# A transformer block with dilated local attention: softmax on tiles transposed by DMA, V scratch kept per block

## The chip, the cores and the metric

The kernel runs on one core of a Trainium2 chip. A core has TensorE (PE in the profile; its weight loads are listed apart as PEld), VectorE (DVE), ScalarE (ACT), GpSimd (POOL) and SyncE (SP), which issues most of the DMA transfers, and sixteen DMA engines that carry them out. The metric is the device time of one execution in microseconds, as the median of several runs.

## The reference

An adaptive layer norm block over x with 2048 positions and 512 channels, bf16: attention with 32 heads of 16 channels in which each position looks at eight earlier ones, two apart, and then a gated feed-forward of width 1792.

```python
mod = (_silu(c) @ w_mod).reshape(c.shape[0], 6, 1, -1)
sa, ca, ga, sb, cb, gb = (mod[:, i] for i in range(6))
h = _layernorm(x) * (1 + ca) + sa
x = x + ga * attention(h)          # below
h = _layernorm(x) * (1 + cb) + sb
x = x + gb * ((gelu(h @ w_gate) * (h @ w_up)) @ w_down)

# attention: W, dil = 8, 2
idx = pos[:, None] - (jnp.arange(W) * dil)[None, :]
kg, vg = k[:, :, idx], v[:, :, idx]              # idx < 0 masked
logits = jnp.einsum('bhsd,bhswd->bhsw', q, kg) * Dh ** (-0.5)
attn = _softmax(jnp.where(idx >= 0, logits, -1e9))
o = jnp.einsum('bhsw,bhswd->bhsd', attn, vg)     # then @ wo
```

## The kernel before, in words

The 2048 positions are worked in four blocks of 512 (sg = 0 to 3). For a block the steps are: layer norm (st, mv, rstd on POOL, xn; L404 to L419), a transposition of xn to channels on partitions (hT; in block 0 by TensorE, L432, in the others by a DMA transposition, L439), scale and shift by the modulation (L447), twelve qkv tiles of four matmuls each (L491) with copies by ScalarE to qT, kT and vT, the logits as products pq = qT * kT shifted by 2w on VectorE (L541) summed over channels by TensorE (LTp, L555), the softmax, the products pv of the probabilities with V on VectorE (L658) summed by TensorE (o_ps, L670), the output projection (x1, L690), the second layer norm and its transposition (h2, also L439), and the feed-forward: g and u (L718), gelu and a copy by ScalarE (L742, L749), their product hh on VectorE (L760), the down projection y (L731) and the store.

In the products pv the four window positions w4 of a group sit on four groups of 32 partitions, so V has to be there four times, each copy shifted by 2*w4 positions. That is done through DRAM: vT is stored to a scratch vscr (L518), and four loads of 32 partitions each read it back with the four shifts into the tile V4 (L527), one run of 520 positions for each of 16 rows of a partition. V4 has one buffer, so the loads of a block wait until the products pv of the block before are done. For block 0, which has nothing before its first position, POOL clears the edge (L240).

The softmax takes the logits LT, with window and head on partitions, transposes them with TensorE into PSUM (LNp, L587), takes the maximum (L598) and subtracts it (z, L607) on VectorE, takes exp on ScalarE (L614), then sum, reciprocal and product on VectorE (L621, L626, L631), transposes back with TensorE (PTp, L640) and copies to PT with ScalarE (L646).

The order of the instructions on every engine is fixed when the program is built. A planner steps through the threads of all blocks; each Op names its engine, a duration, the events it waits for, the buffers it takes and gives back, and the table PR gives each thread a priority. Among the steps that can begin at nearly the same time (within the slack of the engine), the one of lowest priority number goes first. All loads except three are issued by SP from one list (sp_q), mixed with the stores and the DMA transpositions; the first three, c and two parts of w_mod, go through ScalarE's queue. On each queue instructions run strictly in the planned order. PSUM's eight banks are split into four for matmul results (mm), two for attention (att) and two for transposes (tp).

Of the kernel before, what the change touches and what calls it, by code (L numbers as in the profile page):

```python
# [17 lines left out]
PR = {  # L18
    "ga": 28, "mb": 30.4, "gb": -2.8, "wds": 56.8, "wos": 73.9, "ln1": [33.1, 16.9, 32.7, 29.1], "t1": [-35.2,
    55, 3.9, 6.5], "h1": [4.7, 2.3, 4.2, 1], "qkv": [15, 5.4, 30.8, 36], "qev": [40, 53.9, 9, 22.7], "v":  # L20
    [14.4, 70, 13, 46.1], "pq": [7.4, 84.3, 109.8, 154.6], "lmm": [4.5, 21.5, -2.4, 5.1], "lev": [2.2, 19.8,
    38.5, 5.6], "smm": [4.6, 25, 3, -0.9], "soft": [23, 19.5, 1.7, 8.3], "e": [64, 19.2, 103, 16], "ptp": [8,
    7.1, -1.7, 4.8], "pt": [-10.8, 0.2, 10.5, 42.3], "pv": [2.4, 11.1, 71.1, 29.2], "pvmm": [35.5, 31.3, 3.8,
    4.1], "pvev": [-14.5, 64.7, 32.1, 40], "x1mm": [18.6, 1.6, -24.2, -9.1], "x1": [-12.8, 1.5, -0.7, -2],
    "ln2": [28.5, 36.7, 1.4, 68.5], "t2": [1.8, -14.8, 3.9, 0.1], "h2": [-1, 17.3, -2, 10.1], "ffn": [45.9,
    18, 20.7, 56.2], "act": [30.1, -13.5, -2.2, 57.1], "hh": [-5.2, -5.3, 0, 14.6], "st": [150.1, 14.3, 34.2,
    31.2],
# [14 lines left out]
class Op:  # L42


    def __init__(self, eng, w, fn, after=(), take=(), give=(), fire=None, lat=None, act=None, pr=None, dma=None,
                 quad=False):
# [3 lines left out]
        self.quad = quad  # L50


class Planner:
# [5 lines left out]
    def __init__(self):  # L59
        self.clock = {e: 0.0 for e in self.LAT}  # L60
        self.threads = []
        self.done = {}
        self.slack = {"PE": 0.51, "ACT": 0.68, "DVE": 0.14, "POOL": 0, "SP": 0}
        self.far = {"PE": 0, "ACT": 0.05, "DVE": 0.21, "POOL": 0, "SP": 0}
        self.table = None
        self.quad = False
        self.dma = 0.0
        self.log = []
# [4 lines left out]
    def _begin(self, th):  # L73
        op, last = th[2], th[3]
        t = max(self.clock[op.eng], th[4])
        if last is not None:
            t = max(t, last)
        for name in op.after:
# [9 lines left out]
    def run(self):  # L88
# [5 lines left out]
        while live:  # L94
# [27 lines left out]
            if op.dma:  # L122
                self.dma = max(self.dma, t) + (op.lat or 0.0)
                fin = max(end, self.dma) + self.LAT["SP"]
# [4 lines left out]
            if op.fire:  # L129
                self.done[op.fire] = fin  # L130
            self.log.append((t, end, eng, op.fire, th[0]))
# [8 lines left out]
def kernel(  # L140
# [24 lines left out]
    VR = S + VH  # L165

    def pool(name, bufs, **kw):
# [5 lines left out]
          "wm": 1, "hh": 16, "o": 2, "wA": 1, "mm": 4, "att": 2, "tp": 2}  # L173
    pools = {k: pool(k + "_p", NB[k]) for k in NB if k not in ("mm", "att", "tp", "wm")}
    for k in ("mm", "att", "tp"):
# [5 lines left out]
    vscr = dram.tile([P, 4, VR], BF16, name="vscr")  # L181
# [646 lines left out]
```

## Time and profile before

| quantity | value |
|---|---|
| median of 3 runs (lowest, highest) | 254.66 us (254.41, 255.35) |
| profiled execution: its own time | 255.11 us |
| profiled execution: span | 253.2 us |
| busy: PE, DVE, ACT, POOL | 240.3, 185.2, 144.6, 15.3 us |
| granted TensorE clock over the span | 0.987 |
| DMA: packets, volume | 37417, 29.41 MB |
| V loads: number and size, median us from issue to landing | 12 of 520 KB, 9.7 |
| first qkv matmul, first pv product | 13.27 us, 49.16 us |

The span is the profiled stretch of the core; the execution's own time is 1.9 us longer. A busy share is the share of the span in which the engine has an instruction under way; matmuls overlap, so a row's count times its mean duration exceeds its busy time. Where a row names "idle before", that is time in which the engine waited, and the name behind the arrow is what ended the wait. The chain is followed back from the last instruction, at each step to what released it. In the rows of SP's queue the duration is the time that the issuing instruction held the queue, not the transfer's.

### The profile page before, as it was taken

Reading aid. Unit: us, or ns where it says so; the run is one execution under the profiler, and the core shown is the slowest. Engines: PE = TensorE matmul, PEld = TensorE weight load, DVE = VectorE, ACT = ScalarE, POOL = GpSimd, SP = SyncE. Lnnn points to the kernel's source line nnn. Section 1 sums busy time; section 2 is a strip of 40 time slices with the busy share of each in tenths; the row PEclk is TensorE's granted clock in tenths of the full one; section 3 lists DMA queues with packets and bytes.
Section 4 is the critical chain, followed back from the end, with each engine's and each line's share of the span. In section 5 each row is a group of like instructions: output and inputs, shape, how many; then the busy total and the mean of one; then the engine's idle time right before and its main releaser. Section 6 shows DMA issues by size and latency. Waiting matters only on the chain.

```text
span 253.2 us, 3608 instructions
## 1 busy us (share of the span) xinstructions
PE 240.3 (95%) x1353; PEld 105.2 (42%) x1353; DVE 185.2 (73%) x295; ACT 144.6 (57%) x237; POOL 15.3 (6%) x37
## 2 busy tenths in 40 slices
PE   6789698899999999999999999999999999999994
PEld 2444334434443433444444334444344444444441
DVE  3499949999999999999999969688948422222221
ACT  2065459978569967430796763448654730766400
POOL 3410003000200000002000001000001000000000
PEclk9799979999999999999999999999999999999999
DMA  6999899999983500973300069510000401000011
GB/s 213 350 332 283 166 193 188 356 346 255 198 190 116 183 0 0 203 137 71 81 16 1 0 129 197 116 43 23 0 0 3 84 21 52 11 4 0 0 41 41
DMA packets 37417, 29.41 MB, mean 116 GB/s; under 512 B 15512, under 2 KB 36248, under 8 KB 37400
## 3 DMA queue, kind: packets, MB, share of 16 engines
q1 hardware_dynamic: 36336, 28.14, 47.2%
q10 hardware_dynamic: 1064, 1.05, 1.3%
q8 instruction: 10, 0.16, 0.3%
q14 instruction: 7, 0.06, 0.1%
HBM read 21.32 MB, written 4.19 MB: 101 GB/s over the span
## 4 chain that ended last, share of the span: by engine, by line
PE 71%; DMA 14%; DVE 7%; ACT 5%; SPq 1%; issue 1%; DVEq 0%; ACTq 0%
PE y_ps L731 19%; PE g_ps L718 19%; PE u_ps L718 19%; DMA wm<-in_w_mod_dram 5%; PE x_ps L690 5%; PE qkv_ps L491 4%; PE o_ps L670 3%; DMA x<-in_A_x_dram 3%; DMA hT<-xn 3%; DMA h<-xn 2%; DVE st L404 2%; DVE pq L541 2%; ACT hT L447 1%; PE LTp L555 1%; ACT h L447 1%; DVE xn L419 1%
## 5 line engine op out<-in xcount | busy, mean ns | idle before, releaser
L718 PE MATMUL g_ps<-h,Wg 128*128 128x512 bf16 x224 | 57.9, 379 | 0.6 <-ACT h L447 0.3
L718 PE MATMUL u_ps<-h,Wu 128*128 128x512 bf16 x224 | 57.6, 379 | 0.0
L491 PE MATMUL qkv_ps<-hT,wqkv 128*128 128x512 bf16 x192 | 47.3, 390 | 3.9 <-ACT hT L447 2.6
L731 PE MATMUL y_ps<-WdP,hht 128*128 128x512 bf16 x224 | 49.3, 379 | 0.0
L742 ACT ACTIVATE gl<-g_ps 128x512 bf16<-128x512 f32 x56 | 33.5, 599 | 26.7 <-PE g_ps L718 23.3
L749 ACT CAST ub<-u_ps 128x512 bf16<-128x512 f32 x56 | 33.0, 588 | 20.2 <-PE u_ps L718 20.2
L760 DVE TENSOR_TENSOR hht<-gl,ub 128x512 bf16<-128x512 bf16 x56 | 23.5, 420 | 28.1 <-ACT ub L749 27.5
L658 DVE TENSOR_TENSOR pv<-PT,V 128x2048 bf16<-128x2048 bf16 x32 | 37.8, 1219 | 1.0 <-ACT PT L646 1.0
L541 DVE TENSOR_TENSOR pq<-qT,kT 128x2048 bf16<-128x2048 bf16 x32 | 37.8, 1216 | 0.4 <-ACT kT L508 0.4
L718 PEld LDWEIGHTS <-Wg 128*128 128x128 bf16 x224 | 21.1, 98 | 28.5 <-issue 4.6
L731 PEld LDWEIGHTS <-hht 128*128 128x128 bf16 x224 | 21.8, 98 | 26.4 <-issue 0.4
L718 PEld LDWEIGHTS <-Wu 128*128 128x128 bf16 x224 | 21.1, 98 | 27.7 <-issue 4.0
L491 PEld LDWEIGHTS <-wqkv 128*128 128x128 bf16 x192 | 20.9, 115 | 26.5 <-issue 9.8
L404 DVE BATCH_NORM_STATS2 st<-x 128x6 f32<-128x512 bf16 x32 | 21.7, 680 | 6.4 <-DMA x<-in_A_x_dram 6.3
L767 DVE TENSOR_TENSOR ot<-y_ps,x 128x512 bf16<-128x512 f32 x16 | 11.0, 687 | 21.1 <-PE y_ps L731 21.1
L413 POOL TENSOR_TENSOR rstd<-rstd,neghalf 128x4 f32<-128x4 f32 x8 | 10.7, 1340 | 178.9 <-DVE rstd L409 178.9
L447 ACT ACTIVATE h<-h,modT,scl 128x512 bf16<-128x512 bf16 x16 | 11.7, 803 | 7.1 <-DMA h<-xn 7.0
L690 PE MATMUL x_ps<-woP,oT 128*128 128x512 bf16 x64 | 15.6, 379 | 0.0
L508 ACT CAST kT<-qkv_ps 128x512 bf16<-128x512 f32 x16 | 9.2, 586 | 5.8 <-PE qkv_ps L491 5.8
L419 DVE TENSOR_SCALAR xn<-x,mv,rstd 128x512 bf16<-128x512 bf16 x32 | 11.4, 408 | 1.6 <-POOL rstd L413 1.5
L512 ACT CAST vT<-qkv_ps 128x512 bf16<-128x512 f32 x16 | 9.4, 588 | 5.2 <-PE qkv_ps L491 5.1
L699 DVE TENSOR_TENSOR x<-x_ps,x 128x512 bf16<-128x512 f32 x16 | 10.8, 683 | 1.7 <-PE x_ps L690 1.5
(62 smaller groups left out, 157.7 us busy)
## 6 DMA issues: line engine op xcount, KB each, us to landing
V<-vscr SPq DMA_DIRECT2D x12, 520.0 KB, 9.7
wm<-in_w_mod_dram SPq DMA_DIRECT2D x4, 512.0 KB, 9.8
vscr<-vT SPq DMA_DIRECT2D x4, 512.0 KB, 7.1
out_dram<-ot SPq DMA_DIRECT2D x16, 128.0 KB, 1.7
Wg<-in_B_w_gate_dram SPq DMA_DIRECT2D x1, 1792.0 KB, 7.5
Wu<-in_B_w_up_dram SPq DMA_DIRECT2D x1, 1792.0 KB, 11.9
WdP<-in_B_w_down_dram SPq DMA_DIRECT2D x1, 1792.0 KB, 7.5
wqkv<-in_A_wqkv_dram SPq DMA_DIRECT2D x3, 512.0 KB, 7.4
```

The lines of the kernel that those rows point to most:

```text
L404: nc.vector.bn_stats(out=st_k["st"][:, c4, :], in_=src()[:, c4, :])
L419: nc.vector.tensor_scalar(out=B[key][:, c4, :], in0=src()[:, c4, :], scalar1=st_k["mv"][:, c4, 0:1], scalar2=st_k["rstd"][:, c4:c4 + 1], o ...
L447: nc.scalar.activation(out=h, in_=h, func=ACT.Identity, scale=sc(dt), bias=bi(dt))
L491: nc.tensor.matmul(ps[:].rearrange("p (c k) -> p c k", k=P), lhsT=wqkv[:, dt, blk * D + j:(blk + 1) * D:4], rhs=B["hT", sg][:, :, dt, :], ...
L541: nc.vector.tensor_tensor(out=pq[:], in0=_ap(B["qT", sg][:, j, :], [[0, 4], [1, SG]]), in1=_ap(kT[:, j, k0:k0 + SG], [[2, 4], [1, SG]]), o ...
L658: nc.vector.tensor_tensor(out=t[:], in0=_ap(B["PT", sg][:, wg, :], [[0, 4], [1, SG]]), in1=B["V4", sg][:, :, j, c0:c0 + SG], op=ALU.mult)
L690: nc.tensor.matmul(ps[:], lhsT=B["oT", sg][:, j, c4 * P:(c4 + 1) * P], rhs=woP[:, j, :], start=(j == 0), stop=(j == 3))
L718: nc.tensor.matmul(ps[:].rearrange("p (c k) -> p c k", k=P), lhsT=Wt[:, dt, ft * P:(ft + 1) * P], rhs=B["h2T", sg][:, :, dt, :], start=(dt ...
L731: nc.tensor.matmul(ps[:], lhsT=B["hh", sg, ft][:, c4 * P:(c4 + 1) * P], rhs=B["WdP"][:, ft, :], start=(ft == 0), stop=(ft == FT - 1))
L742: nc.scalar.activation(out=gl[:], in_=B["g", sg, ft][:], func=ACT.Gelu_apprx_tanh)
L749: nc.scalar.copy(out=ub[:], in_=B["u", sg, ft][:])
L760: nc.vector.tensor_tensor(out=hh[:], in0=B["gl", sg, ft][:], in1=B["ub", sg, ft][:], op=ALU.mult)
```

## The change

Five things are changed together.

1. **V scratch.** Every block has a scratch of its own, vscr[sg], with a halo of 16 positions in front (VL = 528 positions a row). POOL writes the halo into vT (zeros for block 0, the last 16 positions of the block before for the others; vhalo), the store writes the whole tile, and each of the four loads reads a partition's 16 rows as one contiguous stretch of 8448 - 2*w4 elements and writes it 2*w4 elements further on. The loads pass max_dma_last_dim=4 * VL.
2. **Softmax.** LT is transposed by a DMA transposition on SP (soft_in), not by TensorE, into a bf16 tile LN in SBUF; maximum and sum are trees of elementwise operations in three levels; subtraction, exp and the product with the reciprocal work in place; the result goes back by a second DMA transposition (soft_out).
3. **PSUM.** The pool tp is gone; mm has five banks and att three.
4. **Loads and weights.** wqkv lies in SBUF by its three parts; the loads are several threads with priorities of their own (q_head, q_wo, q_x, q_mb, q_gu, q_gb, q_d), all on SP except c.
5. **Head.** x of block 0 comes in two loads, its layer norm is finished in two halves, its transposes are ordered by halves (transp0), warm-up matmuls are moved and three are added. The planner has new priorities, slacks and durations; a step with hold keeps SP occupied until its transfer is over.

The diff, without the table of priorities and without edits that only carry names:

```diff
@@ Planner._begin
+        if op.dma:
+            t = max(t, self.lanes[0])
@@ Planner.run
-                fin = max(end, self.dma) + self.LAT["SP"]
+                if op.hold:
+                    end = self.clock[eng] = max(end, self.dma)
+                fin = max(end if not op.hold else 0.0, self.dma) + self.LAT["SP"]
+                self.lanes = self.lanes[1:] + [fin]
...
-    VR = S + VH
+    VL = SG + VH
-          "wm": 1, "hh": 16, "o": 2, "wA": 1, "mm": 4, "att": 2, "tp": 2}
+          "wm": 1, "hh": 16, "o": 2, "wA": 1, "mm": 5, "att": 3, "ln": 1, "PT": 1}
-    vscr = dram.tile([P, 4, VR], BF16, name="vscr")
+    vscr = [dram.tile([P, 4, VL], BF16, name=f"vscr{g}") for g in range(NSG)]
-    wqkv = pools["wA"].tile([P, DT, 3 * D], BF16, name="wqkv", tag="wA")
+    wqkv = pools["wA"].tile([P, 3, DT, D], BF16, name="wqkv", tag="wA")
...
+        def q_head():
+            yield Op("SP", 0.45, ldx(0, 0, 1), fire="x0.0", lat=mb(0.125))
+            yield Op("SP", 0.45, ldx(0, 1, 4), fire="x0.1", lat=mb(0.375))
+            yield Op("SP", 0.5, ldwm(1), take=[SL[WM[1]]], fire="wm1", lat=mb(0.5))
+            yield Op("SP", 0.5, ldwm(0), take=[SL[WM[0]]], fire="wm0", lat=mb(0.5))
+            yield Op("SP", 0.5, ldq(0), fire="wqkv0", lat=mb(0.5))
+            yield Op("SP", 0.5, ldq(1), fire="wqkv1", lat=mb(0.5))
+            yield Op("SP", 0.5, ldx(1), fire="x1", lat=mb(0.5))
+            yield Op("SP", 0.5, ldq(2), fire="wqkv2", lat=mb(0.5))
+            yield Op("SP", 0.5, ldx(ORDER[2]), fire=f"x{ORDER[2]}", lat=mb(0.5))
+        def q_wo():
+            yield Op("SP", 0.5, ldwm(2), take=[SL[WM[2]]], fire="wm2", lat=mb(0.5), after=["LN1.1.t!"])
             for i in range(4):
+                yield Op("SP", 0.5, ld(woP[H * i:H * i + H, :, :], wo_v[i]), fire=f"wo{i}", lat=mb(0.125))
+        def q_x():
+            yield Op("SP", 0.5, ldx(ORDER[3]), fire=f"x{ORDER[3]}", lat=mb(0.5), after=["LN1.1.t!"])
+        def q_mb():
+            yield Op("SP", 0.65, ldwm(3), take=[SL[WM[3]]], fire="wm3", lat=mb(0.5), after=["V4ld.0!"])
+            yield Op("SP", 0.65, ldwm(4), take=[SL[WM[4]]], fire="wm4", lat=mb(0.5))
+        def q_gu():
+            yield Op("SP", 0.65, ld(Wg[:], wg_v), fire="Wg", lat=mb(1.8), after=["V4ld.0!", f"LN1.{ORDER[2]}.t!"])
+            yield Op("SP", 0.65, ld(Wu[:], wu_v), fire="Wu", lat=mb(1.8))
+        def q_gb():
+            yield Op("SP", 0.65, ldwm(5), take=[SL[WM[5]]], fire="wm5", lat=mb(0.5), after=["V4ld.0!", "wm2!"])
...
     def vload(sg):
-            nc.sync.dma_start(out=vscr[:, :, VH + sg * SG:VH + (sg + 1) * SG], in_=B["vT", sg][:])
+            nc.sync.dma_start(out=vscr[sg][:], in_=B["vT", sg][:])
         for w4 in range(4):
             def f(w4=w4):
-                z = 0 if sg else 8 + 2 * w4
-                src = bass.AP(vscr.tensor, vscr.offset + VH + sg * SG - 8 - 2 * w4 + z,
-                              [[16 * VR, H], [VR, 16], [1, SG + 8 - z]])
-                nc.sync.dma_start(
-                    out=B["V4", sg][H * w4:H * w4 + H, :, :, z:SG + 8].rearrange("p i j s -> p (i j) s"), in_=src)
-            yield Op("SP", 0.65, f, after=[f"vst.{sg}", "M2"], take=[SL["v4"]] if w4 == 0 and sg else [],
-                     fire=f"V4.{sg}.{w4}" if w4 < 3 else f"V4ld.{sg}", lat=2.8)
+                t, n = B["V4", sg], 4 * 4 * VL
+                d = t[H * w4:H * w4 + H, :, :].rearrange("p r s -> p (r s)")
+                src = bass.AP(vscr[sg].tensor, vscr[sg].offset, [[n, H], [1, n - 2 * w4]])
+                nc.sync.dma_start(out=d[:, 2 * w4:n], in_=src, max_dma_last_dim=4 * VL)
+            yield Op("SP", 0.65, f, after=[f"vst.{sg}"], take=[SL["v4"]] if w4 == 0 else [],
+                     fire=f"V4.{sg}.{w4}" if w4 < 3 else f"V4ld.{sg}", lat=1.7)
...
+    def soft_in(sg):
+            B["LN", sg] = T("ln", [P, 2 * CPS, P], BF16, "LN")
+            nc.sync.dma_start_transpose(out=B["LN", sg][:], in_=B["LT", sg][:].rearrange("p g s -> p (g s)"))
+        yield Op("SP", 1.15, f, after=[f"lt.{sg}.0", f"lt.{sg}.1"] + (["lm.0"] if sg == 0 else []), take=[SL["ln"]],
+                 give=[SL["lt"]], fire=f"ln.{sg}", lat=1.0, hold=True)
     def soft(sg):
+        def view(g):
+            return B["LN", sg][:, g * CPS:(g + 1) * CPS, :].rearrange("p c (w h) -> p c w h", h=H)
+        def over_w(t):
+            return _ap(t[:, :, 0, :], [[4 * H, CPS], [0, 4], [1, H]])
+        def tree(t, op):
+            nc.vector.tensor_tensor(out=t[:], in0=view(0), in1=view(1), op=op)
+            nc.vector.tensor_tensor(out=t[:, :, 0:2, :], in0=t[:, :, 0:2, :], in1=t[:, :, 2:4, :], op=op)
+            nc.vector.tensor_tensor(out=t[:, :, 0, :], in0=t[:, :, 0, :], in1=t[:, :, 1, :], op=op)
...
+            tree(B["mt", sg], ALU.max)
...
+            for g in range(2):
+                nc.vector.tensor_tensor(out=view(g), in0=view(g), in1=over_w(B["mt", sg]), op=ALU.subtract)
...
+            e = B["LN", sg]
+            nc.scalar.activation(out=e[:], in_=e[:], func=ACT.Exp)
...
+            B["sm", sg] = smp["sm"].tile([P, CPS, 4, H], F32, name="sm")
+            tree(B["sm", sg], ALU.add)
...
+                nc.vector.reciprocal(out=B["mt", sg][:, :, 0, :], in_=B["sm", sg][:, :, 0, :])
...
+            for g in range(2):
+                nc.vector.tensor_tensor(out=view(g), in0=view(g), in1=over_w(B["mt", sg]), op=ALU.mult)
+    def soft_out(sg):
+            B["PT", sg] = T("PT", [P, 2 * CPS, P], BF16, "PT")
+            nc.sync.dma_start_transpose(out=B["PT", sg][:], in_=B["LN", sg][:].rearrange("p g s -> p (g s)"))
+        yield Op("SP", 1.15, f, after=[f"p.{sg}"], take=[SL["PT"]], give=[SL["ln"]], fire=f"pt.{sg}", lat=1.0, hold=True)
...
+    def vhalo(sg):
+        def f():
+            if sg == 0:
+                nc.gpsimd.memset(B["vT", 0][:, :, 0:VH], 0.0)
+            else:
+                nc.gpsimd.tensor_copy(out=B["vT", sg][:, :, 0:VH], in_=B["vT", sg - 1][:, :, SG:VL])
```

## The prediction

> **What bounds the kernel now.** I read the page first, then the chain of waits, then windows by stage, then SP's timeline, because the change sends more through SP's DMA queue. The page:
>
> ```profile
> span 253.2 us, 3608 instructions
> ...
> PE 240.3 (95%) x1353; PEld 105.2 (42%) x1353; DVE 185.2 (73%) x295; ACT 144.6 (57%) x237; POOL 15.3 (6%) x37
> ...
> DMA packets 37417, 29.41 MB, mean 116 GB/s; under 512 B 15512, under 2 KB 36248, under 8 KB 37400
> ...
> q10 hardware_dynamic: 1064, 1.05, 1.3%
> ...
> PE 71%; DMA 14%; DVE 7%; ACT 5%; SPq 1%; issue 1%; DVEq 0%; ACTq 0%
> ```
>
> The chain is 71% TensorE. Stretches of it (columns: stretch, its length, busy time of PE, PEld, DVE, ACT and POOL, granted clock, DMA share, GB/s):
>
> ```profile
> 32.80:36.30 3.50, 3.50 (x15) 1.34 (x12) 0.84 (x3) 1.73 (x4) 0.00 (x0) 0.54 1.13 198
> 83.60:249.80 166.20, 166.07 (x888) 71.69 (x887) 113.35 (x182) 91.32 (x148) 3.86 (x3) 1.00 0.24 52
> 107.00:112.00 5.00, 5.00 (x25) 2.29 (x24) 4.82 (x10) 2.37 (x4) 0.00 (x0) 1.00 1.11 196
> 198.90:201.70 2.80, 2.80 (x15) 1.27 (x14) 0.57 (x2) 1.94 (x4) 0.00 (x0) 1.00 1.00 187
> ```
>
> From 83.6 to 249.8 TensorE idles 0.1 us of 166, so work taken from it there is worth its length, and any wait put into it costs its length. Before 83.6 it waits for data. After a wait the clock is 0.54 for 3.5 us (first line), a loss of about 1.7 us. The last two lines price DMA packets, below. SP's queue (start, time on the queue, line):
>
> ```profile
> 21.59 5.22 SPq L439 DMA_TRANSPOSE hT<-xn  x1
> 27.13 2.65 SPq L527 DMA_DIRECT2D V<-vscr  x4
> 43.26 0.57 SPq L256 DMA_DIRECT2D Wg<-in_B_w_gate_dram  x1
> 43.89 0.50 SPq L256 DMA_DIRECT2D Wu<-in_B_w_up_dram  x1
> ...
> 48.17 8.95 SPq L439 DMA_TRANSPOSE hT<-xn  x1
> 57.20 0.55 SPq L518 DMA_DIRECT2D vscr<-vT  x1
> ```
>
> A transposition holds SP until it is nearly done: 8.95 us for the one behind Wg and Wu, which no later issue passes. Undisturbed it is short (last column, us to landing):
>
> ```profile
> h<-xn SPq DMA_TRANSPOSE x4, 4.3
> hT<-xn SPq DMA_TRANSPOSE x3, 7.3
> ```
>
> So transfers on this queue finish in order, and a long one delays all behind it.
>
> **The parts with small prices.** TensorE loses 64 transposes (L587, L640); on the chain eight of them are a 0.45 us piece, five such pieces lie after 83.6: -2.3 us. VectorE's softmax per block is now 2 x 0.684 + 2 x 0.689 + 1.875 + 0.951 + 1.215 = 6.8 us; after it is two trees (one 128x512 bf16 operation each at the 0.42 of hht plus two smaller at 0.2 to 0.3, the float32 one nearer 0.7), four halves at 0.42 and the reciprocal 0.95: about 4.7. That saves 8 us of an engine that is 73% busy, beside TensorE. ScalarE loses four PT copies of 1.0 us, also beside. POOL's memsets and its three halo copies are under 0.4 us each on an engine that is 6% busy. A fifth bank for matmuls and a third for attention remove the waits of L718 for ScalarE (0.2 us). The head (x in two loads first, then wm, then wqkv) lets the first qkv matmul start, I estimate, at 11.5 instead of 13.3 us. In it wm1 and wm0 move from ScalarE's queue (0.95 us of issues) to SP's, gB's memset from POOL (0.53) to VectorE, and three warm-up matmuls of 0.43 are added: their cover is TensorE's wait for x, and without it they would cost 1.3. wm2, the four wo and x3 move behind the transposition hT.1 (six issues of 0.6 on SP, 1.5 MB), which nobody needs before 28 us, except that the first V store now stands behind them. Were this all, the time would fall by 4 us.
>
> Added to SP's queue are eight transpositions of 256 KB. They hold SP for 1 to 1.8 us each and land 3 to 4.3 us after issue, from half and whole of the h row. LN and PT now queue behind whatever SP issued before them.
>
> **The part with a large price: the V loads (after: L560).** The limit max_dma_last_dim=4*VL is 2112 and counts bytes, so a run holds at most 1056 elements. Each load's row of 8448 - 2*w4 elements is cut into equal runs under that limit. In the program as built, w4=0 has 8 runs of 1056, w4=1 has 41 of 206, w4=3 has 9 of 938. For w4=2 the row is 8444 = 4 x 2111 elements, and 2111 is prime: 2111 runs of 4 elements, 8 bytes each, on 32 partitions. That is 67,552 runs, once per block.
>
> Does each run become a packet? In the trace it does, one per row of a pattern: x, wm, wqkv, vscr, V, WdP and out have 2048 + 3072 + 1536 + 2048 + 8192 + 1792 + 2048 = 20,736 rows of about 1 KB, and the page has 36,248 - 15,512 = 20,736 packets between 512 B and 2 KB. No transfer there has runs adjacent on both sides, so the trace can't exclude merging. The Trainium skill ("DMA: Bandwidth & Descriptors", "Why a DMA increments its semaphore by 16 and not by 1") says that one descriptor moves one contiguous run of the last dim, and warns of a long row cut into equal pieces with no fitting divisor. That speaks against this load; no run here shows it yet.
>
> Price of a packet. Transpositions, 256 B: the window at 198.9 has 2.8 us x 16 engines x 1.00 / 2048 packets = 21.9 ns. Queue q10, 987 B: 1.3% of 16 x 253.2 us / 1064 = 49.5 ns. The line through both gives 12.5 ns at 8 B. V loads, 1040 B, shifted against their destination: the window at 107 has 5 x 16 x 1.11 us / 942 packets (196 GB/s) = 94 ns, that is 44.5 more than q10's. So an 8-byte run costs between 12.5 ns, if the shift costs per byte, and 57 ns, if it costs per packet; 21.9 is the nearest row from above. Cheaper than the line is possible too, since 8 B lies outside its rows. I take 15 ns, near the line because a shift of so few bytes has little to double, and above it because these are tiny reads of DRAM, which no row shows. All 16 engines share the work, as the shares of 1.00 show: 67,552/16 = 4222 packets, **T = 63 us** per load (53 and 240 at the ends).
>
> The Trainium skill (same page, "Why small descriptors are slow (HBM only)") prices a 256 B packet at 8 + 3 cycles; an estimate by it for one beat is 4 cycles, 4/11 of 21.9 = 8 ns, T = 34 and the sum below 401.
>
> **What T stops.** The issue order of SP in the changed program decides. Block 0: vscr store, V load w4=0, transposition LN.0, V loads w4=1, 2, 3, wm5, transposition hT.2, wm3, wm4, transposition PT.0, Wg, Wu, hT.3. So the first T delays qkv of block 2, mod1 and PT.0, hence pv.0; TensorE has only qkv.1 meanwhile. Each later block has its V loads directly ahead of the h2 transposition of the block before (w4=2 of block 1 ahead of h2 of 0, and so on), and V4 has one buffer, so its loads also wait for the last pv. TensorE holds one finite stage each time; then FFN waits. The four T are therefore in series, and the sum is of what lies between them:
>
> - Start to first T: hT.1's transposition at 19 (20.2 + 1.4 of xn in the trace, less the head's 2); its 1.8 on SP, six issues of 0.6; store issued 24.4, behind 1.5 MB at 301 GB/s (5 us), lands 31; LN.0 to 34.5; w4=1 3.0: **38**.
> - After T1: w4=3 3.0, wm5 1.6, hT.2 2.8, wm3 and wm4 3.2, PT.0 1.4, issue and landing 3.5: pv.0 15.5 later. Beside it vscr 1.7, Wg and Wu 10.8, hT.3 2.8, then w4=0 1.5 and w4=1 3: **38** in all.
> - After T2: w4=3 3, vscr 1.7, LN.1 1.4, h2 4.3, exp with its table 2.3, scaling 0.8: FFN.0 14 later; PT.1 and then eight pv and eight hht on VectorE, 8 x (1.22 + 0.42) = 13.1, end 33.5 later; V loads 7: **40.5**.
> - After T3: 3 + 4.3 + 3 to FFN.1, LN.2 and softmax to PT.2 at 24.5, pv 9.8, LN.3 and issue 1.2, V loads 7: **42.5**.
> - After T4: 3 + 4.3 + 3.2: **10.5**. Then TensorE's rest: two FFN of 28 x 0.865 + 12.1 = 36.3, 4.5 of y.1, o 2.6, x1 3.5: **83.2**, and the tail 253.2 - 249.7 = **3.5**.
>
> That is 256.2; four restarts at half clock add 4 x 1.7 = 6.8: 263. Span = 263 + 4 x 63 = **515**. The profiled execution took 255.11, 1.9 outside its span; it stood 0.45 above the median of 254.66. Forecast 515 + 1.9 - 0.4 = **516.5 us**.
>
> **Rivals.**
> 1. Adjacent runs merge, and the third load costs what its neighbours do (3 us). Then only the small parts count: 254.7 - 4 = 250.5, **faster**. Place: V load w4=2. It decides where a run costs under about 1.2 ns (T under 5 us, the slack that V loads had: landing at 39, pv.0 at 49.2). For it: the runs lie adjacent on both sides. Against: the packet count. 3%.
> 2. They merge, but PT.0 waits behind hT.2, wm3 and wm4: pv.0 at 53.5 + 3 against 49.2, +7, less 2.3 and some cover: **258**. 3%.
> 3. The shift costs per packet: T = 240, **1225**. For it: the 94 ns. Against: 44.5 ns is about what doubles the 1 KB row, so it looks like a price per byte. 5%.
> 4. Later transfers pass the slow one, so it delays only pv: the first T whole, the others less the 19 us until FFN reaches its first o: 263 + 63 + 3 x 44 = **458**. Against: the 8.95 us hold. 5%.
> 5. The forecast's mechanism: 84%, with its price open from 7 to 34 ns for most of that: 7 ns (T = 28) gives 377, 34 ns (T = 142) gives 833.
>
> **Numbers.** Range **375 to 830**: below lie rivals 1 and 2 (6%) and cheaper runs (4%), above rival 3 and runs over 34 ns (9%). The mechanism's own range at 9 to 25 ns is 415 to 685. No change means within 0.5%, about 1.3 us, what a measurement of this kernel can tell. Faster 0.03 (rival 1), same 0.01 (between rivals 1 and 2), slower 0.96.
>
> **What would show it.** Right: over 300,000 packets under 512 B; DMA share near 1 but single-digit GB/s in four stretches of equal length T; hT, h2 and PT waiting tens of us for their transpositions, SP held there; TensorE idle in those stretches, and its clock low after each. The small parts: no LNp or PTp rows, mx and the sum as trees, DVE busy about 8 us less without hht changing. Wrong: about 37,000 packets, V loads landing in 10 us. Wrong in size: another T, read directly as issue to landing of the third load; or stretches that overlap TensorE's work more than summed.

## The result and the profile after

The changed kernel takes **401.31 us** (median of 4 runs) against 255.0 before, measured beside it: 1.570 times as long, with a 95% interval of 1.558 to 1.583. The ratio leaves out the one execution of the four that ran in a slower state (410.68 us, clock 0.791). The profiled execution took 400.77 us and has a span of 398.9. The predicted point was 516.5 with a range of 375 to 830: the sign and the mechanism came out as forecast, the size 115 us too high.

The page of the changed kernel, with the lines that answer to those shown of before:

```profile
span 398.9 us, 3496 instructions
...
PE 246.1 (62%) x1276; PEld 103.2 (26%) x1292; DVE 178.7 (45%) x313; ACT 141.8 (36%) x233; POOL 16.2 (4%) x37
...
GB/s 264 158 230 170 15 14 14 21 248 380 222 33 14 14 14 216 99 138 114 15 14 14 55 113 67 61 72 15 14 14 122 42 29 31 22 41 13 1 15 39
DMA packets 313737, 31.75 MB, mean 80 GB/s; under 512 B 299384, under 2 KB 311032, under 8 KB 313720
...
SPq 50%; PE 27%; DMA 9%; DVE 7%; ACT 4%; issue 2%; POOL 0%; DVEq 0%; ACTq 0%
SPq L560 46%; PE u_ps L735 7%; PE g_ps L735 7%; PE y_ps L748 7%; DVE pv L675 3%; SPq L462 3%; DMA x<-in_A_x_dram 2%; PE qkv_ps L515 2%; DMA LN<-LT 2%; DMA h<-xn 2%; DVE pq L573 1%; DMA wm<-in_w_mod_dram 1%; DMA hT<-xn 1%; ACT h L470 1%; PE o_ps L687 1%
```

TensorE has about as much work as before (240.3 us), in a span 146 us longer. The chain is no longer TensorE's: half of it is SP's queue, and 46% one line, L560, the V loads. The number of packets rose from 37,417 to 313,737. In the trace's packet records 270,208 of them have 8 bytes: 4 x 67,552, as the prediction counted for w4=2. In the row of GB/s the four groups of 14 and 15 are the four stretches in which these loads move half a megabyte each.

SP's queue in the same kernel (start, time on the queue, line):

```profile
31.72 0.33 SPq L560 DMA_DIRECT2D V<-vscr  x1
32.99 1.24 SPq L614 DMA_TRANSPOSE LN<-LT  x1
34.29 43.84 SPq L560 DMA_DIRECT2D V<-vscr  x3
...
103.61 46.88 SPq L560 DMA_DIRECT2D V<-vscr  x4
...
180.04 46.53 SPq L560 DMA_DIRECT2D V<-vscr  x4
...
255.97 46.67 SPq L560 DMA_DIRECT2D V<-vscr  x4
```

In every block SP is held for about 44 to 47 us at the V loads, and whatever stands behind them is not issued. TensorE's longest waits, one in each block (start, length of the work that follows, and in brackets the wait and what ended it):

```profile
85.01 0.61 PE L354 MATMUL mb_ps<-wm,scT 128*128 128x512 bf16 x1 [41.45 <-DMA wm<-in_w_mod_dram]
...
160.75 0.62 PE L587 MATMUL LTp<-pq,Mph 128*32 128x512 bf16 x4 [37.82 <-DVE pq L573]
...
233.89 2.00 PE L735 MATMUL g_ps<-h,Wg 128*128 128x512 bf16 x3 [27.01 <-ACT h L470]
...
310.15 2.70 PE L735 MATMUL g_ps<-h,Wg 128*128 128x512 bf16 x4 [30.22 <-ACT h L470]
```

Together 136.5 us. The first is wm5, queued on SP behind the slow load; the second is pq of a later block, which stands on VectorE behind the softmax that waits for LN.1; the last two are the feed-forward behind the h2 transposition. The stretches of the four slow loads and those between them (stretch, its length, busy time of PE, PEld, DVE, ACT and POOL, granted clock, DMA share, GB/s):

```profile
39.70:78.80 39.10, 3.86 (x18) 1.81 (x16) 10.62 (x19) 5.03 (x8) 2.30 (x2) 0.60 1.87 14
78.80:110.50 31.70, 22.63 (x156) 8.56 (x159) 16.81 (x19) 15.07 (x27) 0.00 (x0) 0.74 1.09 274
110.50:151.10 40.60, 12.43 (x64) 6.20 (x62) 6.57 (x13) 6.46 (x11) 2.10 (x2) 0.69 1.81 15
151.10:186.10 35.00, 24.78 (x131) 9.26 (x132) 26.79 (x39) 20.12 (x33) 0.00 (x0) 0.77 0.67 158
186.10:227.20 41.10, 20.67 (x110) 8.45 (x109) 15.60 (x30) 6.43 (x11) 1.91 (x1) 0.81 1.79 16
227.20:262.30 35.10, 26.80 (x143) 10.29 (x146) 25.50 (x41) 20.76 (x33) 0.00 (x0) 0.83 0.54 97
262.30:303.30 41.00, 17.59 (x81) 7.79 (x80) 11.99 (x29) 7.93 (x12) 1.05 (x1) 0.76 1.80 16
303.30:398.90 95.60, 84.59 (x399) 37.04 (x405) 35.51 (x64) 41.04 (x68) 1.04 (x1) 0.94 0.16 36
```

The slow loads take T = 39.1, 40.6, 41.1 and 41.0 us: 9.3 to 9.7 ns per packet on each of 16 engines. A share of 1.8 means that the packets of an engine overlap: by the packet records one is under way for 17.3 ns on average, but a new one starts every 9.7 or less.

### The profile page after: what moved, and what is told of

Its sections match the earlier page's. It is cut to its first block, busy times and chain, and to the rows that moved or that the text cites. A ratio compares the mean times of both kernels' runs of the same rounds, so it can differ in the third digit from the quotient of the medians.

```text
span 398.9 us, 3496 instructions
## 1 busy us (share of the span) xinstructions
PE 246.1 (62%) x1276; PEld 103.2 (26%) x1292; DVE 178.7 (45%) x313; ACT 141.8 (36%) x233; POOL 16.2 (4%) x37
## 4 chain that ended last, share of the span: by engine, by line
SPq 50%; PE 27%; DMA 9%; DVE 7%; ACT 4%; issue 2%; POOL 0%; DVEq 0%; ACTq 0%
SPq L560 46%; PE u_ps L735 7%; PE g_ps L735 7%; PE y_ps L748 7%; DVE pv L675 3%; SPq L462 3%; DMA x<-in_A_x_dram 2%; PE qkv_ps L515 2%; DMA LN<-LT 2%; DMA h<-xn 2%; DVE pq L573 1%; DMA wm<-in_w_mod_dram 1%; DMA hT<-xn 1%; ACT h L470 1%; PE o_ps L687 1%
## 5 line engine op out<-in xcount | busy, mean ns | idle before, releaser
L735 PE MATMUL g_ps<-h,Wg 128*128 128x512 bf16 x224 | 61.9, 396 | 58.4 <-ACT h L470 57.8
L675 DVE TENSOR_TENSOR pv<-PT,V 128x2048 bf16<-128x2048 bf16 x32 | 37.2, 1221 | 78.2 <-PE LTp L587 41.1
L735 PE MATMUL u_ps<-h,Wu 128*128 128x512 bf16 x224 | 60.0, 392 | 0.0
L515 PE MATMUL qkv_ps<-hT,wqkv 128*128 128x512 bf16 x191 | 46.1, 396 | 1.6 <-DMA wqkv<-in_A_wqkv_dram 1.3
L766 ACT CAST ub<-u_ps 128x512 bf16<-128x512 f32 x56 | 32.9, 587 | 17.4 <-PE u_ps L735 17.3
L470 ACT ACTIVATE h<-h,modT,scl 128x512 bf16<-128x512 bf16 x16 | 11.8, 802 | 72.2 <-DMA h<-xn 72.2
L587 PE MATMUL LTp<-pq,Mph 128*32 128x512 bf16 x128 | 12.4, 457 | 39.0 <-DVE pq L573 39.0
L777 DVE TENSOR_TENSOR hht<-gl,ub 128x512 bf16<-128x512 bf16 x56 | 23.1, 422 | 29.1 <-ACT ub L766 28.9
L626 DVE TENSOR_TENSOR mt<-LN 128x512 bf16<-128x512 bf16 x4 | 1.7, 424 | 71.2 <-DMA LN<-LT 71.2
L354 PE MATMUL mb_ps<-wm,scT 128*128 128x512 bf16 x7 | 3.1, 550 | 43.6 <-DMA wm<-in_w_mod_dram 41.5
L735 PEld LDWEIGHTS <-Wu 128*128 128x128 bf16 x224 | 22.1, 100 | 30.6 <-issue 6.9
L430 POOL TENSOR_TENSOR rstd<-rstd,neghalf 128x4 f32<-128x4 f32 (+1 forms) x9 | 12.2, 1355 | 317.3 <-DVE rstd L426 317.3
L642 ACT ACTIVATE LN<-LN 128x1024 bf16<-128x1024 bf16 x4 | 4.2, 1057 | 40.1 <-DVE LN L637 40.1
L359 ACT CAST gB<-mb_ps 128x512 bf16<-128x512 f32 x2 | 1.2, 586 | 44.9 <-PE mb_ps L354 42.0
```

Of the source, the lines that this page charges most:

```text
L470: nc.scalar.activation(out=h, in_=h, func=ACT.Identity, scale=sc(dt), bias=bi(dt))
L515: nc.tensor.matmul(ps[:].rearrange("p (c k) -> p c k", k=P), lhsT=wqkv[:, blk, dt, j:D:4], rhs=hview(B["hT", sg], dt), start=(dt == 0), st ...
L587: nc.tensor.matmul(LTp[32 * w4:32 * w4 + 32, :], lhsT=M[:], rhs=B["pq", sg, wg, j][:, 3 - w4, :], start=(j == 0), stop=(j == 3), tile_posi ...
L675: nc.vector.tensor_tensor(out=t[:], in0=_ap(B["PT", sg][:, CPS * wg, :], [[0, 4], [1, SG]]), in1=B["V4", sg][:, j:16:4, c0:c0 + SG], op=AL ...
L735: nc.tensor.matmul(ps[:].rearrange("p (c k) -> p c k", k=P), lhsT=Wt[:, dt, ft * P:(ft + 1) * P], rhs=hview(B["h2T", sg], dt), start=(dt = ...
L766: nc.scalar.copy(out=ub[:], in_=B["u", sg, ft][:])
```

## The experiments

The theory is the prediction's: the 8-byte runs of w4=2 make a load of T, four of these stand in series, and the rest is worth little. The rivals are that the rest of the change costs something too (rival 2), that the slow loads overlap other work (rival 4), and another price for a run.

### Long runs for the third load

```diff
-                nc.sync.dma_start(out=d[:, 2 * w4:n], in_=src, max_dma_last_dim=4 * VL)
+                nc.sync.dma_start(out=d[:, 2 * w4:n], in_=src, max_dma_last_dim=8 * VL)
```

> The changed kernel with the limit on a run of the V loads (L560) at 8*VL bytes instead of 4*VL, nothing else. By that limit the row of 8444 elements of w4=2 is cut into 4 runs of 2111 elements (4222 bytes) instead of 2111 runs of 4; w4=1 keeps its 41 runs of 206. Theory A, the mechanism of the prediction: the 8-byte runs of w4=2 are the whole loss, and what is left of the change is worth its small parts. Then the packets under 512 B fall from 299,384 by 270,208 to about 29,000, no load of V takes over 12 us to land, and the time is the prediction's 250.5 us, 2% faster than before. Theory B, rival 2: the loss of the runs goes, but LN and PT now stand in SP's queue behind other transpositions and loads, pv.0 starts late, and the time is 258 us or more. Theory C: the runs are not the cause (the eight added transpositions or the order on SP's queue are): the time stays above 350 us.

Measured 261.44 us beside 255.48, ratio 1.024 (1.020 to 1.028). One number takes 140 us off the changed kernel, so the cause of nearly all of the loss is shown. But what is left is not 250.5: without the runs the change still costs 6 us, as rival 2 had it in size. Page and TensorE's largest wait of this kernel:

```profile
span 259.9 us, 3512 instructions
...
PE 240.4 (93%) x1292; PEld 103.2 (40%) x1292; DVE 178.4 (69%) x313; ACT 141.9 (55%) x233; POOL 16.1 (6%) x37
...
DMA packets 43145, 31.75 MB, mean 122 GB/s; under 512 B 29176, under 2 KB 39672, under 8 KB 43128
```

```profile
47.97 1.89 PE L354 MATMUL mb_ps<-wm,scT 128*128 128x512 bf16 x4 [7.14 <-DMA wm<-in_w_mod_dram]
```

TensorE is busy for 240.4 us, as before (240.3), and idle for 19.5 instead of 12.9; one wait of 7.1 us for wm5 is about the difference.

### Another way to long runs

Every load starts at column 8, ahead of which nothing is read; the limit stays.

```diff
-                src = bass.AP(vscr[sg].tensor, vscr[sg].offset, [[n, H], [1, n - 2 * w4]])
-                nc.sync.dma_start(out=d[:, 2 * w4:n], in_=src, max_dma_last_dim=4 * VL)
+                src = bass.AP(vscr[sg].tensor, vscr[sg].offset + 8 - 2 * w4, [[n, H], [1, n - 8]])
+                nc.sync.dma_start(out=d[:, 8:n], in_=src, max_dma_last_dim=4 * VL)
```

> The changed kernel with every V load starting at column 8 of its row instead of 2*w4 (the columns before 8 are never read), the limit left at 4*VL bytes. Each row is then 8440 = 8 x 1055 elements, eight runs of 2110 bytes for all four loads, w4=1 too. Theory A (the run length alone decides): as with long runs, 250.5 us, or up to 1 us less because the 41 runs of 412 bytes of w4=1 are gone as well; packets under 512 B fall by 275,456 to about 24,000. Theory B (the queue order costs): 258 us or more, the same as with long runs. Theory C (runs are not the cause): above 350 us.

Measured 261.91 us, ratio 1.025 (1.022 to 1.028): the same as with the higher limit. So it is the length of the runs, not the limit as such, and the 41 runs of 412 bytes of w4=1 are worth nothing that can be seen. This kernel is the base of the others below, but for the next one, which starts from the kernel with the higher limit.

### One slow block

```diff
-                nc.sync.dma_start(out=d[:, 2 * w4:n], in_=src, max_dma_last_dim=4 * VL)
+                nc.sync.dma_start(out=d[:, 2 * w4:n], in_=src, max_dma_last_dim=(4 if sg == 1 else 8) * VL)
```

> The changed kernel with the 8-byte runs left in the loads of block 1 alone (limit 4*VL for block 1, 8*VL for blocks 0, 2 and 3). Write E for the time with long runs in all four blocks. Theory A, the four waits stand in series and nothing hides them: one of them costs a quarter of the whole loss, E + (401 - E)/4, which is 288 us if E is 250.5; TensorE idles for most of the 40 us that the load lasts. Theory B, later transfers pass the slow load or TensorE has other work for half of it (rival 4): E + 22 or less, 273 us. The load itself lasts 40 to 42 us in both.

Measured 300.22 us, 38.8 more than with long runs everywhere (261.44, same chip), and 12.2 over the 288, of which 11 are E itself, 261.4 instead of 250.5. A quarter of the whole loss would be 35. The load ran for 41.1 us, and TensorE waited once for 38.6. So nearly the whole T stands in the path, and rival 4 (22 or less) falls. Four blocks at 38.8 would be 155 and not 140: in the changed kernel the first slow load covers the 7 us wait for wm5 that the kernel with long runs has anyway, and TensorE's waits in the last two blocks are only 27.0 and 30.2 us, since the feed-forward lies beside them (TensorE is busy for 20.7 and 17.6 us of these stretches).

### The price of a packet by its length

```diff
-                nc.sync.dma_start(out=d[:, 8:n], in_=src, max_dma_last_dim=4 * VL)
+                nc.sync.dma_start(out=d[:, 8:n], in_=src, max_dma_last_dim=(8, 16, 40, 80)[sg] if w4 == 2 else 4 * VL)
```

> The changed kernel with all V loads from column 8, and in each block another run length for w4=2: 8 bytes in block 0, 16 in block 1, 40 in block 2, 80 in block 3 (2110, 1055, 422 and 211 runs on 32 partitions: 67,520, 33,760, 13,504 and 6,752 packets). It prices a packet by its length. Theory A, a fixed price per packet of 9.6 ns on each of 16 engines (0.6 ns per packet for all of them): 40.5, 20.3, 8.1 and 4.1 us. Theory B, a line through 9.6 ns at 8 B and the 94 ns at 1040 B of the shifted V loads of before: 9.6, 10.3, 12.2 and 15.5 ns, so 40.5, 21.7, 10.3 and 6.5 us. Theory C, the price is per byte moved: each load takes the same 40 us. Total time by A: about 250 + 37 + 18 + 6 + 2 = 313 us, by C about 400 us.

The four loads in windows of this kernel (columns as above, the last one is GB/s; by the packet records each load begins and ends some 0.5 us later than its window):

```profile
39.70:78.70 39.00, 1.19 (x6) 0.40 (x4) 11.25 (x21) 3.19 (x6) 2.14 (x2) 0.57 1.85 16
110.60:131.20 20.60, 13.24 (x67) 6.60 (x66) 7.26 (x15) 7.27 (x13) 2.10 (x2) 0.91 1.74 34
165.90:176.50 10.60, 10.60 (x50) 4.68 (x48) 9.57 (x21) 5.33 (x9) 1.80 (x1) 1.00 1.65 79
212.00:218.30 6.30, 6.30 (x31) 2.88 (x30) 5.61 (x14) 4.93 (x7) 0.00 (x0) 1.00 1.56 117
```

By the packet records the loads last 39.1, 20.6, 10.7 and 6.4 us, that is 9.3, 9.8, 12.7 and 15.1 ns per packet for 8, 16, 40 and 80 bytes. Theory B fits; A is too low at 40 and 80 bytes, and C is out. The whole took 318.15 us, 56.2 over its base; the loads of 40 and 80 bytes lie wholly beside a TensorE that is never idle (10.60 of 10.60 and 6.30 of 6.30).

### Does the shift cost anything at 8 bytes

```diff
-                nc.sync.dma_start(out=d[:, 8:n], in_=src, max_dma_last_dim=4 * VL)
+                nc.sync.dma_start(out=d[:, 8:n], in_=src, max_dma_last_dim=8 if w4 == sg else 4 * VL)
```

> All V loads from column 8, and in block 0 the load w4=0 in 8-byte runs, in block 1 w4=1, in block 2 w4=2, in block 3 w4=3, the others in runs of 2110 bytes. The rows of these four loads lie 0, 4, 8 and 12 bytes apart, modulo 16, between source and destination. It tells whether the shift, which doubles the price of a 1 KB row, costs anything at 8 bytes. Theory A, the shift costs per byte: all four loads take 39 to 41 us, as w4=2 did. Theory B, it costs per packet: the unshifted one takes about half, 20 us, the shifted ones 40. Total time by A about 401 us, by B about 381 us.

The loads last 38.9 us without a shift and 43.9, 40.9 and 41.2 with shifts of 4, 8 and 12 bytes; the whole took 404.91. Theory B, a price per packet, falls: the unshifted load is not half as long. Each shift stands in another block here, and the blocks differ by themselves: shifted by 8 bytes, the load took 39.1 us in block 0 and 40.6, 41.1 and 41.0 in blocks 1 to 3 of the changed kernel. Block by block, no shift saves 0.2 us, 12 bytes cost 0.2, and 4 bytes cost 3, in one run. That a shift is what makes the rows of 1 KB dear is not tested by any run.

### Which resource sets the 9.7 ns

The slow load of block 1 is halved by rows, and the halves are issued by two engines.

```diff
+                if (sg, w4) != (1, 2):
                     nc.sync.dma_start(out=d[:, 8:n], in_=src, max_dma_last_dim=4 * VL)
+                    return
+                for q, eng in enumerate((nc.sync, nc.scalar)):
+                    half = bass.AP(src.tensor, src.offset + 16 * q * n, [[n, 16], [1, n - 8]])
+                    eng.dma_start(out=t[H * w4 + 16 * q:H * w4 + 16 * q + 16, :, :].rearrange("p r s -> p (r s)")[:, 8:n],
+                                  in_=half, max_dma_last_dim=8)
```

> All V loads from column 8 with long runs, but in block 1 the load w4=2 in 8-byte runs, its first 16 rows issued by SP and its last 16 by ScalarE's queue at the same time (33,760 packets each); to be compared with block 1 alone slow on SP's queue, where the load ran 41.1 us and held SP as long. Theory A, the 16 DMA engines set the 9.7 ns per packet: they are shared, and both halves together still take 39 to 42 us. Theory B, the one queue that makes the descriptors sets it, at 0.6 ns each: the halves run at once and end after 20 to 22 us, and SP is held that long; the whole kernel then takes about 280 us instead of 300.

Measured 303.58 us; both halves together take 43.4 us. By the packet records the halves run at once, at equal rates. The single queue doesn't set the time: theory B falls. What both queues share remains: the 16 DMA engines, the memory that they read and write, or a common maker of descriptors; no run here tells these apart. The issues in this kernel, on SP's and ScalarE's queue:

```profile
69.53 0.70 SPq L565 DMA_DIRECT2D V<-vscr  x1
70.27 45.74 SPq L561 DMA_DIRECT2D V<-vscr  x1
```

```profile
70.24 0.67 ACTq L565 DMA_DIRECT2D V<-vscr  x1
```

A load of 33,760 packets is issued in 0.7 us on either queue. What is held, for 45.7 us, is the next issue on SP, here an ordinary load of long runs.

### The 6 us that remain: moving V's store and loads

SP's queue in the base kernel:

```profile
21.91 0.89 SPq L272 DMA_DIRECT2D wm<-in_w_mod_dram  x1
22.85 1.92 SPq L259 DMA_DIRECT2D woP<-in_A_wo_dram  x4
24.81 0.42 SPq L265 DMA_DIRECT2D x<-in_A_x_dram  x1
25.35 0.44 SPq L551 DMA_DIRECT2D vscr<-vT  x1
31.61 0.34 SPq L560 DMA_DIRECT2D V<-vscr  x1
32.03 1.24 SPq L614 DMA_TRANSPOSE LN<-LT  x1
33.32 1.75 SPq L560 DMA_DIRECT2D V<-vscr  x3
35.17 0.40 SPq L272 DMA_DIRECT2D wm<-in_w_mod_dram  x1
36.17 11.77 SPq L462 DMA_TRANSPOSE hT<-xn  x1
```

V is complete at 18.6 us, and its store is issued at 25.35, behind six issues that the change moved there. Then V, wm5 and the transposition hT.2 follow, which holds SP for 11.8 us. Three kernels move steps in the planned order, with the rest of the order kept (each entry: this step, directly behind that one):

```diff
-            op.fn()
+            self.seq.append((op.eng, op.fire, op.fn))
...
+        for what, behind in MOVES:
+            n = [q[1] for q in pl.seq]
+            step = pl.seq.pop(n.index(what))
+            pl.seq.insert([q[1] for q in pl.seq].index(behind) + 1, step)
+        for _, _, fn in pl.seq:
+            fn()
```

```diff
+MOVES = (('vst.0', 'vh.0'),)
```

> The kernel with all V loads from column 8 (261.9 us), and in it one step moved: the store of block 0's V is issued ahead of the transposition hT.1 instead of behind hT.1, wm2, the four wo and x3. V is complete at 18.6 us there, its store is issued at 25.35, and TensorE later idles 7.4 us (to 48.2) for wm5 and then hT.2, which stand behind block 0's V loads. Theory A, the six issues that the change put ahead of the store cost that wait: the store is issued near 19, the load w4=0 near 25 instead of 31.6; the other three stay behind the transposition LN.0, which waits for LT until 32, so about one load's 3 us of the 7.4 is saved: 259 us. Theory B, the DMA engines are full from 25 to 48 whatever the order: 261.5 to 262.5 us.

Measured 261.00 us (ratio 1.023, 1.018 to 1.027): nothing that can be told from 261.9. TensorE's wait for wm5 shrank from 7.4 to 5.3 us, but the one for wm2, whose transfer now shares the engines with the store, grew from 1.9 to 3.2.

```diff
+MOVES = (('vst.0', 'vh.0'), ('V4.0.1', 'V4.0.0'), ('V4.0.2', 'V4.0.1'), ('V4ld.0', 'V4.0.2'), ('wm5', 'V4ld.0'))
```

> As the store ahead of hT.1, and besides all four V loads of block 0 and wm5 are issued ahead of the transposition LN.0 instead of three loads and wm5 behind it. Theory A: the loads move in 25 to 37 us, wm5 lands near 39 and hT.2 near 40 instead of 48, TensorE's wait of 7.4 us goes, and 261.9 - 7.4 = 254.5 us remain. That would show that the part of the change outside the V runs is held up by the order of SP's queue, and is worth no more than 1 us with the order mended. Theory B: LN.0 now lands after the V loads, the softmax and pv.0 of block 0 start later, and 3 us or more of the gain are lost again: 257.5 us or more.

Measured 265.69 us (1.040, 1.035 to 1.045), 3.8 worse. The wait for wm5 fell to 1.9 us, and two of 4.7 and 5.0 us took its place, both for pq of block 1. The first stands on VectorE behind the softmax of block 0, which waits 7.4 us for LN.0, now behind V. The second has another cause, told with the last order below. Theory B.

```diff
+MOVES = (('vst.0', 'vh.0'), ('V4.0.1', 'V4.0.0'), ('V4.0.2', 'V4.0.1'), ('V4ld.0', 'V4.0.2'), ('wm5', 'V4ld.0'), ('wm3', 'wm5'), ('wm4', 'wm3'))
```

> As the loads and wm5 ahead of LN.0, and besides wm3 and wm4 are issued directly behind wm5, ahead of LN.0 and hT.2 instead of behind hT.2. They end two more waits of TensorE in the kernel with long runs (1.2 and 0.9 us at 52 to 54 us). Theory A: these go too: 254.5 - 2 = 252.5 us, faster than the kernel before by 1%. Theory B: LN.0 and hT.2 now stand behind 1 MB more, 3.3 us at 300 GB/s, and qkv of block 2 begins later by as much: 256 us or more.

Measured 269.63 us (1.055, 1.051 to 1.059): the same two waits, now 7.5 and 5.0 us. Theory B again. In the base the DMA share is above 1 from 25 to 60 us but for a part of 30 to 35 (0.57 there), so that what is gained for one transfer is lost for another. That is not all: from 50 to 55 us of the second order the share is 0.44, and TensorE is busy for 0.6 us, while VectorE is busy for 4.8.

### The 6 us that remain: using the empty stretch

One stretch of the base kernel is not full; the first line is the kernel before, the second the base (columns as in the windows above):

```profile
16.00:20.00 4.00, 4.00 (x20) 1.96 (x18) 3.89 (x8) 2.83 (x5) 1.03 (x1) 1.00 1.09 291
```

```profile
16.00:20.00 4.00, 4.00 (x21) 2.08 (x19) 3.06 (x8) 2.62 (x5) 2.03 (x2) 1.00 0.00 0
```

The change had put wm2, the four wo and x3 behind hT.1, whose xn is ready at 19.8. The next kernel puts them back.

```diff
+MOVES = (('wm2', 'x2'), ('wo0', 'wm2'), ('wo1', 'wo0'), ('wo2', 'wo1'), ('wo3', 'wo2'), ('x3', 'wo3'))
```

> The kernel with all V loads from column 8 (261.9 us), and in it the six issues that the change had moved behind the transposition hT.1 (wm2, the four wo, x3; 1.5 MB) put back ahead of it, behind x2; nothing else. In that kernel the DMA engines stand still from 16 to 20 us (share 0.00) and are full from 25 to 60, and moving issues within the full stretch won nothing (261.0, 265.7 and 269.6 us). Theory A, the 1.5 MB moved out of the empty stretch into the full one are what the rest of the change loses: the waits of TensorE for wm2 (1.9 and 0.7 us near 27) go, V's store is issued near 22 instead of 25.4, the LT copies and the V loads come 2 to 3 us earlier, and with them wm5 and hT.2: 261.9 - 2.6 - 3 = 256 us. Theory B, the transposition LN.0, which holds SP until LT is there, and the three V loads behind it set wm5 and hT.2 whatever lies before: only the 2.6 us go or not even these: 259 to 262 us.

Measured 259.14 us (1.015, 1.012 to 1.018): 2.8 us back, inside theory B's range, at its edge. The waits for wm2 are gone; TensorE still waits 6.0 us for wm5 behind V.

```diff
-MOVES = (('wm2', 'x2'), ('wo0', 'wm2'), ('wo1', 'wo0'), ('wo2', 'wo1'), ('wo3', 'wo2'), ('x3', 'wo3'))
+MOVES = (('wm2', 'x2'), ('wo0', 'wm2'), ('wo1', 'wo0'), ('wo2', 'wo1'), ('wo3', 'wo2'), ('x3', 'wo3'),
+         ('wm5', 'vst.0'), ('wm3', 'wm5'), ('wm4', 'wm3'), ('V4ld.0', 'LN1.2.t'))
```

> As the six issues put back, and besides wm5, wm3 and wm4 are issued directly behind V's store, ahead of the first V load, and the last V load of block 0 behind hT.2. The time in which SP waits for LT then carries 1.5 MB, and hT.2 stands behind two V loads instead of three and wm5. Theory A: hT.2 lands near 40 instead of 48, TensorE's waits for wm5, wm3 and wm4 (7.4, 1.2, 0.9 us) shrink to 2 or 3 us in all: 250 to 252 us, faster than before by 1.5 to 2%. Theory B: LN.0, a transposition on the same queue, lands behind these loads, and VectorE's softmax, which stands ahead of pq of block 1, delays TensorE as it did with the loads ahead of LN.0: 258 us or more.

Measured 257.31 us (1.007, 1.004 to 1.010): the best with the change's parts, and still 0.7% slower than before. The waits for wm5, wm3 and wm4 are gone. Two for pq stand in their place; ahead of the first, VectorE's softmax waits 3.4 us for LN.0 among the loads:

```profile
43.52 0.40 PE L590 MATMUL LTp<-pq,Mph 128*32 128x512 bf16 x4 [3.11 <-DVE pq L576]
...
49.11 0.62 PE L590 MATMUL LTp<-pq,Mph 128*32 128x512 bf16 x4 [5.20 <-DVE pq L576]
```

```diff
-         ('wm5', 'vst.0'), ('wm3', 'wm5'), ('wm4', 'wm3'), ('V4ld.0', 'LN1.2.t'))
+         ('wm5', 'vst.0'), ('wm3', 'wm5'), ('wm4', 'wm3'), ('V4.0.0', 'LN1.2.t'), ('V4.0.1', 'V4.0.0'),
+         ('V4.0.2', 'V4.0.1'), ('V4ld.0', 'V4.0.2'))
```

> As the kernel with six issues put back and wm5, wm3, wm4 directly behind V's store (257.3 us), but all four V loads of block 0 are issued behind both transpositions, LN.0 and hT.2, so that neither stands behind or among V loads. In that kernel LN.0, issued at 30.7, lands at 38.6 among three V loads, the softmax is 3.4 us late, and TensorE idles 3.1 and 5.2 us for pq of block 1 behind it; hT.2, issued at 35.4, lands at 43.9. Theory A, it is V's loads on the same queue that hold both transpositions: LN.0 lands near 34, hT.2 near 38, both waits go, and 257.3 - 8 = 249 to 251 us, faster than before by 1.6 to 2.4%. Theory B: V now lands only near 50 and PT.0 behind it, so pv.0 begins at 52 or later as in the kernels so far (49.2 before), and VectorE's late start is passed on to TensorE: 255 us or more.

Measured 260.91 us (1.021, 1.019 to 1.023). Theory A's first half came true: LN.0 no longer makes VectorE wait. Then its second half failed as theory B says, now at the other transposition:

```profile
45.86 0.62 PE L590 MATMUL LTp<-pq,Mph 128*32 128x512 bf16 x4 [4.91 <-DVE pq L576]
56.98 0.62 PE L690 MATMUL o_ps<-pv,Msum 128*32 128x512 bf16 x4 [4.69 <-DVE pv L678]
```

PT.0, issued at 43.45 behind all of V, made VectorE wait for 7.6 us, and pv.0 began at 55.7 (49.2 before). The first of the two waits has no transfer behind it. VectorE works from 27.6 to 48.1 us without a wait that the profile lists; three of its lines in this kernel:

```profile
38.99 1.22 DVE L576 TENSOR_TENSOR pq<-qT,kT 128x2048 bf16<-128x2048 bf16 x1
...
43.30 1.37 DVE L440 TENSOR_SCALAR xn<-x,mv,rstd 128x512 bf16<-128x512 bf16 x4
44.59 3.49 DVE L576 TENSOR_TENSOR pq<-qT,kT 128x2048 bf16<-128x2048 bf16 x3
```

Between the first pq of block 1 and the second it is planned to do sum, reciprocal and product of block 0's softmax and an xn, 5.6 us in all, and TensorE waits for the second. The same 5.6 us lie between these two in the base and in the orders whose second wait was 5.0 and 5.2 us.

What the seven orders show together: TensorE's wait in block 0 can be moved, from wm5 and hT.2 to LN.0 or PT.0, but in none of them did it go away. Two causes lie behind it. One is the softmax's transpositions on SP's queue, as the waits for LN.0 and PT.0 show; the kernel before does these two transposes on TensorE, at 0.45 us for eight, and needs no queue for them. The other is the planned order, which no move on SP's queue changes: in all seven TensorE takes the sums LTp of block 1 ahead of block 2's qkv, while in the kernel before they stand behind it, at 65.5 us. In the base the second pq is done at about 48.4 (47.26 + 1.2), so TensorE, which waits until 48.19 for wm5, would have waited as long without wm5. How the 6 us divide is open: a kernel with the old softmax and the new loads was not run, nor one with the old order on TensorE, nor were the trees and the PSUM banks taken alone.

## Why the prediction was right and where it was wrong

- **Right: the runs.** 8,444 elements cut into 2,111 runs of 8 bytes on 32 partitions, not merged, all 16 engines at work: 270,208 packets of 8 bytes were counted, and longer runs took 140 of the 146 us away. Rival 1's condition (runs merge) fell. That one descriptor moves one contiguous run is also what the Trainium skill says ("DMA: Bandwidth & Descriptors", "Why a DMA increments its semaphore by 16 and not by 1"); the packet count agrees.
- **Right: four loads in series**, with the victims named (mod1 and qkv of block 2, then h2 and LN). One alone costs 38.8 us of its 41.1; TensorE's waits in the last two are some 10 us shorter.
- **Wrong: the price of a run.** The step took 15 ns, between 12.5 (the line through 256 and 987 bytes) and 57; measured are 9.3 to 9.7, below the lower end. The rows of the line multiply the DMA share by the time and divide by the packets, which gives the time that a packet is under way; it is the price only where an engine has one packet at a time, as at 256 bytes (share 1.00). At 8 bytes a packet is under way for 17.3 ns, more than the 15, but 1.8 of them at once, where "DMA share near 1" was forecast. So the term that was mis-sized is the overlap. With the length the time under way changes little (17.3, 16.6, 18.9 and 21.2 ns at 8, 16, 40 and 80 bytes, 21.6 for a transposition's 256), while the price falls from 15.1 ns at 80 bytes to 12.7 at 40 and 9.8 at 16. "Above it because these are tiny reads of DRAM" had no row behind it. That the shift does not double the price of such a packet was right. For the same reason the stretches show 14 to 16 GB/s and not single digits. Four times 63 less four times 40.5 is 90 us of the 116 us by which the span was missed.
- **Wrong in size: the stretches between.** 263 was summed, 237 is measured (398.9 less 161.8). By part, predicted and measured: start to T1 38 and 39.7; T1 to T2 38 and 31.7; T2 to T3 40.5 and 35.0; T3 to T4 42.5 and 35.1; after T4 with TensorE's rest and the tail 97.2 and 95.6; the 6.8 of the clock, put on top of the sum, lies in the measured parts. The three stretches between slow loads are 19 us too long. The step that failed there is the time from a slow load to the last pv: transfers and steps that run at once were added one behind the other. After T3, PT.2 was put 24.5 us on; it was issued at 242.62, 15.4 after T3, because LN.2 goes out directly behind h2's transposition. After T2 the last pv was put at 33.5 and ended at 28.9. After T1, PT.0 was put behind 10.6 us of transfers and was issued after 7.3; besides, the terms given for that stretch add up to 35.3 and not 38, and to 31.8 without PT.0's 3.5 us of landing, beside which the next transfers run.
- **Wrong: "were this all, the time would fall by 4 us."** It rises by 6. The step that failed is the one that costed the six issues behind hT.1 at nothing ("which nobody needs before 28 us, except that the first V store now stands behind them"). Put back, they are worth 2.8 us. The cover it named, V loads landing at 39 well ahead of pv, was true for pv and overlooked wm5 and hT.2, which stand behind V on the same queue. Rival 2 had the right queue and nearly the right price: pv.0 at 56.5 and 258 us, against 54.8 and 261.4. But the wait of 7.1 us is for wm5 and not for pv.0, and the planned order of pq and LTp behind it stands in neither text.
- **The small terms.** VectorE's busy time fell by 6.5 us (8 predicted), with hht all but unchanged (23.5 and 23.1). The first qkv matmul starts at 10.66 us (11.5 predicted), but in the base with long runs at 12.2. Both lie off the path, and no saving in the total was seen from them. In rival 5 two products are off: 7 ns make T 29.6 us and not 28, 34 ns make 143.5 and not 142; nothing rests on them.
- **The estimate by the skill's page** ("Why small descriptors are slow (HBM only)": 32-byte beats and 3 cycles for each packet) came to 401 us, and 401.3 was measured. That is two errors that cancel: it had T = 34 and the stretches at 263; they are 40.5 and 237. Scaled by the 21.9 ns of a 256-byte packet, its rule gives 8, 8, 10 and 12 ns for 8, 16, 40 and 80 bytes; measured are 9.3, 9.8, 12.7 and 15.1. A fixed part is there, as the rule has it, but the rule is 14 to 21% too cheap here, scaled as it is from a transposition's packet: that one moves within SBUF, and the section is on transfers with HBM.

## What to carry to other kernels

Before a long contiguous row goes to a DMA under a limit on its last dimension, factor the length of each row and count the runs: three of these four loads were harmless, and the fourth had a prime factor of 2111. When pieces of work are moved past a step on a queue, ask who stands behind the last of them, not only who needs the moved ones, and whether the DMA engines stand idle in the stretch that they leave. When a wait is to be taken away, look for what would end it next: the wait for wm5 here covered one of the same length for VectorE. A sum of what follows a stall should go by the longest of the paths that run at once, since added one behind the other they made 19 us too much here.

## What was not expected of the hardware

- A packet of 8 bytes costs 9.3 to 9.7 ns of an engine's time, and one of 16 bytes hardly more (9.8); 40 bytes cost 12.7 and 80 bytes 15.1. The first two are under way for about 17 ns, more than one at a time on an engine, so that the DMA share reads 1.8.
- A load of tens of thousands of packets is issued in 0.7 us; the next issue on that queue is held until it is nearly drained (45.7 us). Splitting it over two queues changes neither its time (43.4 against 41.1 us) nor the hold on SP.
- A shift between source and destination hardly matters to 8-byte packets: in block 0 the load took 38.9 us without a shift and 39.1 with 8 bytes, in block 3 41.2 with 12 bytes and 41.0 with 8. Only the one with 4 bytes stands out, 43.9 against 40.6 in block 1; one run each.
